# Sparse attention and MoE: value-row transfers between the loads of pairs 2 and 3, `w_in` held back until the last of them, batch 1's preparations late in the first MoE

## The chip, the cores and the metric

The kernel runs on one core of a Trainium2 chip. The metric is the device time of one execution in microseconds. The profile shows one execution taken by the hardware profiler: its span goes from the first to the last instruction, and its own time is a little longer than its span. The engines are called PE (TensorE, matmuls), PEld (its weight loads), DVE (VectorE), ACT (ScalarE), POOL (GpSimd) and SP (SyncE, which here only issues DMAs).

## The reference

Two parts follow each other. First an attention over 4 batches, 8 heads, 768 positions and 64 channels: each query sees the keys within 15 positions of its own, and one summary for each block of 32 keys (the maximum of the keys, the mean of the values).

```python
k_sum = k.reshape(B, H, nb, block, D).max(axis=3)
v_sum = v.reshape(B, H, nb, block, D).mean(axis=3)
scores_l = scale * np.matmul(q, k.transpose(0, 1, 3, 2))      # kept where |i - j| < 16
scores_s = scale * np.einsum('bhsd,bhnd->bhsn', q, k_sum) + np.log(block)
a = softmax(concatenate([masked scores_l, scores_s], -1))
attn_out = np.matmul(a, np.concatenate([v, v_sum], axis=2))
```

Then the heads are laid side by side, x is 3072 tokens by 512, and a feed-forward stage with a swish of learned beta follows:

```python
h = x @ w_in                                   # 512 -> 2048
g = h * (1.0 / (1.0 + np.exp(-beta * h)))
out = g @ w_out                                # 2048 -> 512
```

## The kernel before, in words

**Tiles.** The attention works by batch (4) and pair of heads (4 pairs, called 0 to 3). Queries are taken in tiles of 64; an even tile (parity 0) and an odd one (parity 1) share a window of 128 rows that holds the local keys, and in the rows that are left over the 24 block summaries. So for each pair there are two key arrays in one tile `kw`, and two value arrays, `ve` for the even and `vo` for the odd tiles. Each has 128 partitions, and what lies in its leftover rows must be moved across partitions. This is done by four small DMAs on SP, called the value rows here (L198, L199, L201, L202): 16 rows from `ve` into `vo`, 16 rows from `vo` into `ve`, and the block means `vm` (24 rows) into both.

**Loads.** Batch 0 is loaded as float32 into `hold` tiles by SP and ACT, 384 KB each for k, q and v of a pair (`load3`, L357). Later batches are loaded by GpSimd, which turns them into bf16 on the way, into `st` tiles (192 KB each). The weights `w_in` and `w_out` come by GpSimd in four chunks each of 512 KB in bf16 (`load_w_in`, L342, `load_w_out`, L345). GpSimd also casts or copies every loaded tile (`casts`, L184): k and q into `k_nat` and `q_nat`, v into `ve` and into `vo`.

**The steps of a pair.** `prep_qk` (L208) turns k and q by TensorE into the PSUM tiles `pk` and `pq` (which share two buffers with `vm_ps` and `px`), copies them into `kw` and `q2`, and makes the block maxima `km`. `prep_v` (L191) makes the block means by six matmuls and issues the value rows. `scores` (L244) multiplies queries and keys, takes the exponential on ACT and, from batch 1 on, multiplies by the band on DVE (L264). `av` (L267) multiplies by the values and normalises on DVE (L278, L281). `x_transpose` (L286) turns the result into `xT`.

**The MoE of a batch.** `h_tile` (L301), 16 of them with 8 matmuls each, then `o_part` (L314), 24 of them with 4 matmuls each. `scale_w_out` (L170) divides `w_out` by beta once, on DVE, in 16 instructions of 512 columns. The preparation and the attention of the next batch are put between the tiles of the MoE by `merge` (L327): preparations evenly through the h tiles, scores and `av` through the o parts.

**What sets the order.** SP and GpSimd run in exactly the order of the program. TensorE, DVE and ACT are ordered by the scheduler of the language when the kernel is built, and each runs its list in order. A tile's buffer is reused when its last reader is done. The order on the two hand-ordered queues before the change: on SP all loads of batch 0, then `beta_tmp`, then the value rows of pairs 0 to 3; on GpSimd the casts of pairs 0 to 2, `w_in` chunk 0, the casts of pair 3, three chunks of `w_in`, four of `w_out`, the loads of batch 1's pairs 0 and 1, and then the casts of batch 1.

Of the kernel before, what the change touches and what calls it, by code (L numbers as in the profile page):

```python
# [12 lines left out]
def kernel(  # L13
# [18 lines left out]
    B, H, S, D = q.shape  # L32
    block = 32
    W = 16
    nb = S // block
    QT = 64
    nch = S // P
# [3 lines left out]
    npair = H // 2  # L41
# [120 lines left out]
    beta_tmp = wpool.tile([k2, P], f32, name="beta_tmp")  # L162

    def load_beta():
        beta_ps = ps.tile([P, k2], f32, name="beta_ps", tag="t", bufs=2)
# [4 lines left out]
    def scale_w_out(n):  # L170
        nc.vector.tensor_scalar(out=w_out_sb[:, n], in0=w_out_sb[:, n], scalar1=inv_beta[:, n:n + 1],
                                scalar2=None, op0=ALU.mult)
# [11 lines left out]
    def casts(b, g):  # L184
        nat[(b, g)] = cast_qk("k", b, g), cast_qk("q", b, g)
        ve, vo = ve_bufs[b % 2][:, g], vo_bufs[b % 2][:, g]
        f = staged.pop(("v", b, g)).rearrange("p (h c d) -> p c h d", h=2, d=D)
        nc.gpsimd.tensor_copy(out=ve[:, 0:nch, 0:2 * D].rearrange("p c (h d) -> p c h d", h=2), in_=f)
        nc.gpsimd.tensor_copy(out=vo[:, 1:, 0:2 * D].rearrange("p c (h d) -> p c h d", h=2), in_=f)

    def prep_v(b, g):  # L191
        ve, vo = ve_bufs[b % 2][:, g], vo_bufs[b % 2][:, g]
        vm_ps = ps.tile([P, 2 * D], f32, name="vm_ps", tag="t", bufs=2)
        for c in range(nch):
            nc.tensor.matmul(vm_ps[:], A_avg[:, c, :], ve[:, c, 0:2 * D], start=(c == 0), stop=(c == nch - 1))  # L195
# [105 lines left out]
    def h_tile(b, ni):  # L301
        if ni % 8 == 0:
            h_bufs[(b, ni // 8)] = moe_pool.tile([P, 8, S], bf16, name="h_sb", tag="h_sb", bufs=4)
        big = ps.tile([P, 2, 512], f32, name="h_ps", tag="big", bufs=3)
        for kk in range(2):
            for ki in range(k1):
                nc.tensor.matmul(big[:, kk, 0:MG], w_in_sb[:, ki, ni * P:(ni + 1) * P],  # L307
                                 xT[b][:, ki, kk * MG:(kk + 1) * MG], start=(ki == 0), stop=(ki == k1 - 1))
        nc.scalar.activation(out=h_bufs[(b, ni // 8)][:, ni % 8, :].rearrange("p (k m) -> p k m", k=2),  # L309
                             in_=big[:, :, 0:MG], func=ACTF.Silu, scale=beta_sb[:, ni:ni + 1])  # L310
# [16 lines left out]
    def merge(main, side, span=None):  # L327
        n, m = span or len(main), len(side)
        j = 0
        for i, f in enumerate(main):  # L330
            f()
            while j < m and (j + 1) * n <= (i + 1) * m:
                side[j]()
                j += 1
        while j < m:
            side[j]()
            j += 1

    w_in_r = moe_w_in.rearrange("(a p) n -> p a n", p=P)
    w_out_r = moe_w_out.rearrange("(a p) n -> p a n", p=P)  # L340

    def load_w_in(i, c=d_ff // 4):  # L342
        nc.gpsimd.dma_start(out=w_in_sb[:, :, i * c:(i + 1) * c], in_=w_in_r[:, :, i * c:(i + 1) * c])  # L343
# [16 lines left out]


    load3(0, 2)
    load3(0, 3)
    nc.sync.dma_start(out=beta_tmp[:], in_=moe_beta.rearrange("(a p) -> a p", p=P))
    for g in range(npair):
        casts(0, g)
        if g == 2:
            load_w_in(0)
    for i in range(1, 4):
        load_w_in(i)  # L370
    for i in range(4):
        load_w_out(i)
    prep_qk(0, 0)
    prep_v(0, 0)
    clear_qk(1)
    prep_qk(0, 1)
    both_scores(0, 0)
# [16 lines left out]
    last["norm0"] = last["norm"]  # L394
    load3(1, 0)
    load3(1, 1)

    for b in range(B):
        nxt = b + 1 if b + 1 < B else None
        side_h, side_o = [], []  # L400
        if nxt is not None:
            for g in range(npair):
                def prep(g=g):
                    casts(nxt, g)
                    if g + 2 < npair:
                        load3(nxt, g + 2)
                    prep_qk(nxt, g)
                side_h += [prep, lambda g=g: prep_v(nxt, g)]
# [3 lines left out]
            side_o = list(sc[0])  # L412
            for g in range(1, npair):
                side_o += [sc[g][0], fin[g - 1][0], sc[g][1], fin[g - 1][1], fin[g - 1][2]]
            side_o += fin[npair - 1]
            if nxt + 1 < B:
                side_o[4:4] = [lambda: load3(nxt + 1, 0)]
                side_o[9:9] = [lambda: load3(nxt + 1, 1)]
# [37 lines left out]
```

The softmax here doesn't subtract the row's maximum and nothing guards it: scores larger than these inputs give would overflow.

## Time and profile before

| | |
|---|---|
| median of 3 runs | 262.31 us (261.51 to 264.7) |
| the profiled execution's own time | 263.51 us |
| its span | 261.8 us |
| PE busy | 228.0 us, 87% |
| DVE busy | 153.3 us, 59% |
| ACT busy | 115.6 us, 44% |
| POOL busy | 93.3 us, 36% |
| first stretch of the MoE without waits begins | 50.5 us |
| last piece of batch 1's attention (`px`, TensorE) | 103.05 us |

The busy share of an engine is a mean over stages of different kinds. The first 50 us are the attention of batch 0 alone; from there to about 212 the MoE of batches 0 to 2 runs with the attention of the next batch between its tiles; the rest is the MoE of batch 3. A line of the chain or of a timeline gives the start, the length, the engine, the line of the kernel and the tile written and the tile read; brackets give the idle time before it and what ended it.

### The profile page before, as it was taken

What the parts mean: (1) busy time and instruction counts of PE and PEld (TensorE: products, weight loads), DVE (VectorE), ACT (ScalarE), POOL (GpSimd) and SP (SyncE); (2) the same over time, 40 slices, a digit from 0 to 9 for tenths busy, and PEclk for the clock granted to TensorE, in tenths of its full rate; (3) what the DMA queues carried; (4) which work ended last, traced back from release to release, by engine and by line L of the source; (5) the groups of instructions that cost most, each with busy time, mean ns of one, the idle gap of its engine ahead of it and who ended that gap; (6) DMA issues with size and microseconds to landing.
All of it is one profiled execution on the core that took longest, in us unless ns stands there. A gap on an engine that the chain in (4) does not pass through costs nothing.

```text
span 261.8 us, 4353 instructions
## 1 busy us (share of the span) xinstructions
PE 228.0 (87%) x1681; PEld 138.1 (53%) x1681; DVE 153.3 (59%) x355; ACT 115.6 (44%) x136; POOL 93.3 (36%) x126
## 2 busy tenths in 40 slices
PE   0473866599999879999999999999999999999984
PEld 0262643266665545566665555666655545654431
DVE  7672775669668888266658792666688831001221
ACT  1355641376684320476782331677833306661000
POOL 6679522599999990199510000000000000000000
PEclk9997695789999999999999999999999999999999
DMA  7999999999899999279401111101011111001111
GB/s 180 264 262 148 192 206 201 163 106 112 88 141 148 119 112 155 82 72 119 49 18 74 49 40 62 31 24 25 21 40 71 52 43 40 0 0 43 73 54 73
DMA packets 63667, 24.53 MB, mean 94 GB/s; under 512 B 49808, under 2 KB 60576, under 8 KB 63648
## 3 DMA queue, kind: packets, MB, share of 16 engines
q0 software_dynamic: 41664, 11.28, 42.8%
q1 hardware_dynamic: 18864, 11.82, 16.6%
q10 hardware_dynamic: 3120, 1.18, 2.0%
q8 instruction: 13, 0.21, 0.3%
q14 instruction: 6, 0.05, 0.1%
HBM read 27.27 MB, written 6.29 MB: 128 GB/s over the span
## 4 chain that ended last, share of the span: by engine, by line
PE 68%; DMA 12%; DVE 9%; POOL 5%; SPq 2%; issue 2%; ACT 1%; POOLq 0%; ACTq 0%
PE h_ps L307 32%; PE o_ps L320 25%; DMA st<-in_k_dram 8%; DVE x_nat L281 4%; DMA hold_86<-in_v_dram 4%; DVE attn L264 3%; PE s_ps L259 2%; SPq L83 2%; PE px L292 2%; PE av_ps L276 2%; PE pk L215 2%; PE vm_ps L195 2%; PE pq L235 2%; ACT attn L261 1%; POOL w_in_sb L343 1%
## 5 line engine op out<-in xcount | busy, mean ns | idle before, releaser
L320 PE MATMUL o_ps<-w_out_sb,h_sb 128*128 128x512 bf16 x384 | 92.0, 379 | 0.8 <-DVE o_sb L324 0.8
L307 PE MATMUL h_ps<-xT,w_in_sb 128*128 128x384 bf16 x512 | 91.1, 333 | 0.0
L309 ACT ACTIVATE h_sb<-h_ps,beta_sb 128x768 bf16<-128x768 f32 x64 | 57.5, 900 | 49.8 <-PE h_ps L307 48.9
L307 PEld LDWEIGHTS <-w_in_sb 128*128 128x128 bf16 x512 | 49.8, 99 | 31.6 <-issue 2.0
L320 PEld LDWEIGHTS <-h_sb 128*128 128x128 bf16 x384 | 35.9, 98 | 35.1 <-issue 1.5
L324 DVE COPY o_sb<-o_ps 128x512 f32<-128x512 f32 x24 | 16.6, 690 | 48.7 <-PE o_ps L320 48.4
L261 ACT ACTIVATE attn<-s_ps,bias 128x768 bf16<-128x768 f32 x32 | 28.2, 900 | 34.7 <-PE s_ps L259 26.9
L281 DVE TENSOR_TENSOR x_nat<-av_ps,r 64x384 bf16<-64x384 f32 x64 | 35.5, 555 | 1.5
L276 PEld LDWEIGHTS <-attn 128*128 128x128 bf16 x192 | 14.2, 103 | 16.9 <-issue 6.2
L264 DVE TENSOR_TENSOR attn<-attn,band 128x768 bf16<-128x768 bf16 x24 | 16.1, 671 | 9.9 <-ACT attn L261 9.6
L179 POOL COPY k_nat<-st 128x768 bf16<-128x768 bf16 x12 | 10.9, 908 | 21.5 <-PE pk L215 16.4
L227 DVE TENSOR_REDUCE km<-pk 128x24 bf16<-128x768 bf16 x16 | 15.2, 950 | 5.2 <-ACT kw_139 L225 1.7
L83 POOL DMA_DIRECT2D st<-in_v_dram x12 | 12.5, 1040 | 5.5 <-DMA w_in_sb<-in_moe_w_in_dram 3.2
L215 PEld LDWEIGHTS <-k_nat 128*128 128x128 bf16 x96 | 7.7, 110 | 11.1 <-issue 6.0
L254 PE MATMUL s_ps<-negband,identity 128*128 128x384 bf16 x16 | 6.5, 422 | 7.2 <-DVE negband L129 7.0
L276 PE MATMUL av_ps<-ve_146,attn 128*128 128x129 bf16 x48 | 4.9, 242 | 9.0 <-DMA ve_146<-vm 9.0
L278 DVE RECIPROCAL r<-av_ps 128x6 f32<-128x6 f32 x32 | 6.2, 194 | 10.9 <-PE av_ps L276 10.4
L215 PE MATMUL pk<-identity,k_nat 128*128 128x128 bf16 x96 | 9.3, 239 | 3.1 <-POOL k_nat L179 3.1
L292 PE MATMUL px<-identity,x_nat 128*128 128x128 bf16 x96 | 8.8, 232 | 3.3 <-DVE x_nat L281 2.9
L83 POOL DMA_DIRECT2D st<-in_q_dram x12 | 10.0, 837 | 2.7 <-DMA w_out_sb<-in_moe_w_out_dram 1.8
L235 PE MATMUL pq<-identity,q_nat 128*128 128x128 bf16 x96 | 9.0, 236 | 2.2 <-POOL q_nat L179 1.7
L292 PEld LDWEIGHTS <-x_nat 128*128 128x128 bf16 x96 | 5.9, 103 | 9.4 <-DVE x_nat L281 9.4
(136 smaller groups left out, 240.9 us busy)
## 6 DMA issues: line engine op xcount, KB each, us to landing
out_dram<-o_sb SPq DMA_DIRECT2D x24, 256.0 KB
st<-in_k_dram POOLq DMA_DIRECT2D x12, 192.0 KB, 3.9
st<-in_q_dram POOLq DMA_DIRECT2D x12, 192.0 KB, 4.9
st<-in_v_dram POOLq DMA_DIRECT2D x12, 192.0 KB, 5.7
w_in_sb<-in_moe_w_in_dram POOLq DMA_DIRECT2D x4, 512.0 KB, 8.2
w_out_sb<-in_moe_w_out_dram POOLq DMA_DIRECT2D x4, 512.0 KB, 17.5
hold_84<-in_k_dram SPq DMA_DIRECT2D x3, 384.0 KB
hold_86<-in_v_dram SPq DMA_DIRECT2D x3, 384.0 KB
```

What stands on the lines that cost most here:

```text
L83: eng.dma_start(out=dst, in_=srcs[nm][b, g])
L215: nc.tensor.transpose(pk[:, e, c * P:(c + 1) * P], kt[:, c, e], identity)
L227: nc.vector.tensor_reduce(out=km[:], in_=pk.rearrange("p e (n f) -> p n e f", f=block // NE), op=ALU.max, axis=mybir.AxisListType.XY)
L261: nc.scalar.activation(out=a.rearrange("p (k j) h q -> p k (j h q)", k=2), in_=big[:, :, 0:w], func=ACTF.Exp, bias=bias[:, par:par + 1], s ...
L264: nc.vector.tensor_mul(out=a, in0=a, in1=band[:, par, None, None, :].to_broadcast([P, nch, 2, QT]))
L276: nc.tensor.matmul(ov[:, m // TB, m % TB], a[:, m], vt[:, m], start=True, stop=True)
L281: last["norm"] = nc.vector.tensor_mul(out=x[par * QT:(par + 1) * QT, :, hh, :].rearrange("p (k j) d -> p k j d", k=2), in0=ov[lo:lo + D, : ...
L292: nc.tensor.transpose(px[:, c * P:(c + 1) * P], x[:, c], identity)
L307: nc.tensor.matmul(big[:, kk, 0:MG], w_in_sb[:, ki, ni * P:(ni + 1) * P], xT[b][:, ki, kk * MG:(kk + 1) * MG], start=(ki == 0), stop=(ki = ...
L309: nc.scalar.activation(out=h_bufs[(b, ni // 8)][:, ni % 8, :].rearrange("p (k m) -> p k m", k=2), in_=big[:, :, 0:MG], func=ACTF.Silu, sca ...
L320: nc.tensor.matmul(o_ps, h_bufs[(b, ni // 8)][:, ni % 8, ms * P:(ms + 1) * P], w_out_sb[:, ni, :], start=(ni == 0), stop=(ni == k2 - 1))
L324: nc.vector.tensor_copy(out=o_sb[:], in_=o_ps)
```

## The change

Five things are done.

1. On SP, `beta_tmp` is loaded after the first three loads, and the value rows of pair 0 stand between the loads of pair 2 and the loads of pair 3.
2. On GpSimd, `w_in` chunk 0 is issued after the casts of pair 2, as before; after the casts of pair 3 come `w_in` chunks 1 to 3, then the loads of batch 1's pairs 0 and 1, and the four chunks of `w_out` last (before, `w_out` was ahead of these loads).
3. `w_in` chunk 1 is given a wait for the last value-row transfer of batch 0's pair 3. What follows it on GpSimd follows it in order.
4. `scores` of pairs 2 and 3 of batch 0 are put ahead of `finish` of pairs 0 and 1 in the program.
5. `merge` is replaced by one list of positions. With batch 0's MoE, the four preparations of batch 1 begin at positions 11, 14, 19 and 23 of 40 (16 h tiles, then the scalings of `w_out`, then 24 o parts) in place of one each four h tiles from the start on. With the later MoEs they begin at positions 1, 5, 9 and 13. Scores and `av` stay spread over the first 18 o parts.

```diff
+    beta_tmp = wpool.tile([k2, P], f32, name="beta_tmp")
     load("k", 0, 0, nc.sync)
...
     load("v", 0, 1, nc.scalar)
+    nc.sync.dma_start(out=beta_tmp[:], in_=moe_beta.rearrange("(a p) -> a p", p=P))
...
-        nc.sync.dma_start(out=vo[SUM[1]:SUM[1] + nb, 1:, 0:2 * D], in_=src)
+        last["vw"] = nc.sync.dma_start(out=vo[SUM[1]:SUM[1] + nb, 1:, 0:2 * D], in_=src)
...
     load3(0, 2)
+    for g in range(3):
+        casts(0, g)
+    load_w_in(0)
+    prep_qk(0, 0)
+    prep_v(0, 0)
     load3(0, 3)
-    nc.sync.dma_start(out=beta_tmp[:], in_=moe_beta.rearrange("(a p) -> a p", p=P))
-    for g in range(npair):
-        casts(0, g)
-        if g == 2:
-            load_w_in(0)
-    for i in range(1, 4):
-        load_w_in(i)
+    casts(0, 3)
+    after_vw = [load_w_in(i) for i in range(1, 4)]
+    load3(1, 0)
+    load3(1, 1)
     for i in range(4):
         load_w_out(i)
-    prep_qk(0, 0)
-    prep_v(0, 0)
...
+    both_scores(0, 2)
     finish(0, 0)
-    both_scores(0, 2)
     prep_v(0, 3)
+    tc.add_manual_dep(after_vw[0].ins, last["vw"].ins.name,
+                      mybir.DependencyInfo(mybir.DependencyClass.Sync, mybir.DependencyReason.DATA),
+                      reason="the value rows of batch 0 move ahead of the weights")
+    both_scores(0, 3)
     finish(0, 1)
-    both_scores(0, 3)
...
-    load3(1, 0)
-    load3(1, 1)
...
+            if b == 0:
+                start, step = (11.0, 14.0, k2 + 3.0, k2 + 7.0), 0.5
+            else:
+                start, step = (1.0, 5.0, 9.0, 13.0), 1.0
+            for g in range(npair):
+                side += [(start[g] + step * i, f) for i, f in enumerate(preps[g])]
+            seq = list(sc[0])
             for g in range(1, npair):
-                side_o += [sc[g][0], fin[g - 1][0], sc[g][1], fin[g - 1][1], fin[g - 1][2]]
-            side_o += fin[npair - 1]
+                seq += [sc[g][0], fin[g - 1][0], sc[g][1], fin[g - 1][1], fin[g - 1][2]]
+            seq += fin[npair - 1]
+            side += [(k2 + 1.0 + 18.0 * i / len(seq), f) for i, f in enumerate(seq)]
...
-        merge([lambda ni=ni: h_tile(b, ni) for ni in range(k2)], side_h)
+        main = [lambda ni=ni: h_tile(b, ni) for ni in range(k2)]
         if b == 0:
-            with tc.issue_after(last["norm0"].ins):
-                for n in range(k2):
-                    scale_w_out(n)
-        merge([lambda ms=ms, p=p: o_part(b, ms, p, 4) for ms in range(nch) for p in range(4)],
-              side_o, 18)
+            def scales():
+                with tc.issue_after(last["norm0"].ins):
+                    for n in range(k2):
+                        scale_w_out(n)
+            main.append(scales)
+        main += [lambda ms=ms, p=p: o_part(b, ms, p, 4) for ms in range(nch) for p in range(4)]
+        side.sort(key=lambda z: z[0])
+        for pos, f in enumerate(main):
+            while side and side[0][0] <= pos:
+                side.pop(0)[1]()
+            f()
+        for _, f in side:
+            f()
```

More of the change, by code (lines that the diff above doesn't have):

```diff
@@ L161 @@
     inv_beta = wpool.tile([P, k2], f32, name="inv_beta")
-    beta_tmp = wpool.tile([k2, P], f32, name="beta_tmp")
     def load_beta():
@@ L325, in o_part @@
             nc.sync.dma_start(out=out_r[b * nch + ms], in_=o_sb[:])
[L327 to L337, printed above, removed]
     w_in_r = moe_w_in.rearrange("(a p) n -> p a n", p=P)
@@ L342, in load_w_in @@
     def load_w_in(i, c=d_ff // 4):
-        nc.gpsimd.dma_start(out=w_in_sb[:, :, i * c:(i + 1) * c], in_=w_in_r[:, :, i * c:(i + 1) * c])
+        return nc.gpsimd.dma_start(out=w_in_sb[:, :, i * c:(i + 1) * c], in_=w_in_r[:, :, i * c:(i + 1) * c])
     def load_w_out(i, c=k2 // 4):
@@ L394 @@
     last["norm0"] = last["norm"]
-    load3(1, 0)
-    load3(1, 1)
     for b in range(B):
         nxt = b + 1 if b + 1 < B else None
-        side_h, side_o = [], []
+        side = []
         if nxt is not None:
[L402 to L408, printed above, removed]
+            preps = [[lambda g=g: casts(nxt, g), lambda g=g: prep_qk(nxt, g), lambda g=g: prep_v(nxt, g)]
+                     for g in range(npair)]
+            for g in range(2):
+                preps[g][0:1] += [lambda g=g: load3(nxt, g + 2)]
             sc = [[lambda g=g, u=u: scores(nxt, g, u) for u in range(2)] for g in range(npair)]
@@ L411 @@
                    for g in range(npair)]
-            side_o = list(sc[0])
+            if b == 0:
[5 more added lines that the diff above has]
+            seq = list(sc[0])
             for g in range(1, npair):
-                side_o += [sc[g][0], fin[g - 1][0], sc[g][1], fin[g - 1][1], fin[g - 1][2]]
-            side_o += fin[npair - 1]
+                seq += [sc[g][0], fin[g - 1][0], sc[g][1], fin[g - 1][1], fin[g - 1][2]]
+            seq += fin[npair - 1]
+            side += [(k2 + 1.0 + 18.0 * i / len(seq), f) for i, f in enumerate(seq)]
             if nxt + 1 < B:
-                side_o[4:4] = [lambda: load3(nxt + 1, 0)]
-                side_o[9:9] = [lambda: load3(nxt + 1, 1)]
-        merge([lambda ni=ni: h_tile(b, ni) for ni in range(k2)], side_h)
+                side += [(k2 + 4.0, lambda: load3(nxt + 1, 0)), (k2 + 10.0, lambda: load3(nxt + 1, 1))]
+        main = [lambda ni=ni: h_tile(b, ni) for ni in range(k2)]
         if b == 0:
-            with tc.issue_after(last["norm0"].ins):
-                for n in range(k2):
-                    scale_w_out(n)
-        merge([lambda ms=ms, p=p: o_part(b, ms, p, 4) for ms in range(nch) for p in range(4)],
-              side_o, 18)
+            def scales():
[11 more added lines that the diff above has]
+            f()
 _INS = ['q', 'k', 'v', 'moe_w_in', 'moe_w_out', 'moe_beta']
```

## The prediction

> **What bounds the kernel now.** I read the page first, then the chain of waits in order of time, the table by stretch, the timelines of TensorE, VectorE and GpSimd for the first 110 us, and the groups of single tiles.
>
> From the page, the busy shares:
>
> ```profile
> span 261.8 us, 4353 instructions
> PE 228.0 (87%) x1681; PEld 138.1 (53%) x1681; DVE 153.3 (59%) x355; ACT 115.6 (44%) x136; POOL 93.3 (36%) x126
> ```
>
> TensorE is the bound over the whole, but not everywhere. The chain of waits (start, length, what) shows where it isn't:
>
> ```profile
> 6.76 10.72 DMA hold_86<-in_v_dram
> ...
> 28.16 20.64 DMA st<-in_k_dram
> 48.97 1.48 POOL k_nat L179
> 50.73 3.19 PE h_ps L307 x10
> ...
> 103.05 0.51 PE px L292 x6
> ```
>
> After 50.73 the chain is nearly all TensorE up to the end, with short VectorE pieces at 86 to 99, 144 to 153 and 195 to 211. So what the change can win or lose lies before `px L292` at 103.05: that is the last piece of batch 1's attention, made inside batch 0's MoE, and the later batches follow it like clockwork. I measure everything as a shift of this instant.
>
> The timeline of TensorE (start, length, what, and in brackets the idle time before it with its releaser) shows its waits up to the MoE:
>
> ```profile
> 25.29 0.81 PE L276 MATMUL av_ps<-ve_146,attn 128*128 128x129 bf16 x6 [4.33 <-DMA ve_146<-vm]
> ...
> 40.95 0.81 PE L276 MATMUL av_ps<-ve_146,attn 128*128 128x129 bf16 x6 [3.46 <-DMA ve_146<-vm]
> ...
> 50.50 0.23 PE L215 MATMUL pk<-identity,k_nat 128*128 128x128 bf16 x1 [3.06 <-POOL k_nat L179]
> ```
>
> `av` waits for value rows (9.0 us in three waits, by the table of waits), and the MoE waits until 50.5 for batch 1's first key tile. The timeline of VectorE shows `w_out` scaled just before that, batch 1 begun at 54.34, and in the MoE's second half what casts on GpSimd do to the band multiplication `attn`:
>
> ```profile
> 45.73 4.03 DVE L171 TENSOR_SCALAR w_out_sb<-w_out_sb,inv_beta 128x512 bf16<-128x512 bf16 x15
> 54.34 0.66 DVE L222 COPY kw_138<-pk 128x480 bf16<-128x480 bf16 x1 [4.59 <-PE pk L215]
> ...
> 82.74 0.58 DVE L264 TENSOR_TENSOR attn<-attn,band 128x768 bf16<-128x768 bf16 x1
> ...
> 89.57 2.11 DVE L264 TENSOR_TENSOR attn<-attn,band 128x768 bf16<-128x768 bf16 x1
> ```
>
> The table by stretch (the last two columns are the DMA engines' share and GB/s written) gives the rate of GpSimd's queue, first with weights and then with `st` loads in it:
>
> ```profile
> 30.00:32.00 2.00, 1.10 (x14) 0.80 (x12) 1.17 (x2) 1.99 (x4) 0.76 (x1) 0.97 1.22 201
> ...
> 48.00:50.00 2.00, 0.00 (x0) 0.00 (x0) 1.76 (x7) 0.73 (x1) 1.03 (x1) 1.00 2.09 176
> ```
>
> **What the Trainium skill says.** "DMA: Bandwidth & Descriptors", section Queues, rings and completion order: an engine takes the descriptors of one ring in order, and shares its time by turns among rings. The trace agrees: GpSimd's weights and `st` loads land in the order of issue (`w_in` chunks at 29.9, 33.9 and 37.1, `w_out` at 39.8, 42.9 and up to 47.6, the first `st` at 48.97), and small row transfers take long beside them (issued by 21.6, landed at 25.2). The same page, section Anatomy of one DMA, has a fixed cost of about 2 us; I use that price for rows on a quiet queue, which no row here shows. "SBUF — State Buffer", section Who interferes with whom: a VectorE instruction with two SBUF inputs blocks against a GpSimd instruction that reads SBUF, for its whole length. The `attn` rows agree: 0.58 without, 2.11 with casts running beside it.
>
> **Step 1, rows of pairs 0 to 2.** On SP the four row transfers of pair 0 move ahead of the three loads of pair 3. `vm` is copied at 14.45 to 14.72, so the two that need it issue at 14.8 to 16.5 instead of 20.65 to 22.5, and land by 18.5 instead of 25.2. SP is in order: the three loads queue behind them and issue at 16.5 to 18.1 instead of 10.23 to 16.4. Moved past as well: `beta_tmp`, some 0.6 us earlier on SP, covered by loads in flight.
>
> **Step 2, pair 3 late.** The loads of pair 0 to 2 are 9 x 384 KB; at 265 GB/s from 2.2 us they are over at about 15.6. Pair 3's 1.18 MB start at about 18 and share with `w_in` chunk 0, which GpSimd issues at 17.5: alone they need 4.5 us, with it (2.6 us at 203 GB/s) 7.1. So pair 3's v lands at about 25 (in the kernel before its cast ran at 21.5). TensorE no longer waits for rows at 25.29, but it reaches the `av` of pair 0 at about 25 to 26 anyway, since the built order has all of pair 2's scores and pair 3's transposes ahead of it. The `vm` of pair 3 then follows pair 3's scores and the first `px`: TensorE at 29.8 if the clock stays full, 31.6 at half (before: 33.51).
>
> **Step 3, the hold.** The last row transfer of pair 3 ends its issue at 31.9 to 34.1 and lands 1.8 later, 33.7 to 35.9: middle 34.9. Only then does GpSimd issue `w_in` chunk 1 (before: 23.05). Queued behind it on GpSimd, in this order: two more `w_in` chunks, six `st` loads of batch 1's pairs 0 and 1, four `w_out` chunks, and every cast of batch 1.
>
> **Step 4, the front gain.** Without waits for rows, VectorE paces the end of batch 0's attention: six `av` normalisations of 1.35 (0.20 + 2 x 0.56, with gaps), beta 0.4. From 30.1 to 32.3 that gives 38.7 to 41.2 for the last `px` (before 45.75), and `xT` 0.8 us later. The MoE streams from about 41 rather than 50.5, on `w_in` chunk 0 alone for 32 matmuls; chunk 1, due at 40 to 42, is there in time, since ten matmuls at the half clock (3.35 us, as at 50.56) and 22 at 0.1625 need 6.9 us. By itself this is worth about 8 us (50.5 less 9 matmuls of 0.16 already done is 49.0, against 41).
>
> **Step 5, the queue.** From 34.9, 7 chunks x 0.524 MB and 6 x 0.197 MB are 4.85 MB. At 203 GB/s (rows of 28 to 44 us) 23.9 us, plus 1.0 because `st` loads ran at 176, plus 1.6 to start and 0.7 to finish: the last `w_out` chunk lands at 34.9 + 27.2 = 62.1. Before it landed at about 47.6 (issued 27.4, at most 20.2 to landing). Bounds: 59.5 to 65.
>
> **Step 6, what waits for it.** In the built order of the changed kernel VectorE has all 16 `w_out` scalings ahead of the first copy of batch 1's pair 0. In the kernel before that cost nothing, since `w_out` was there before `k_nat`. Now the last four scalings (0.27 each) end at 63.2 and VectorE stands idle from about 41 to there, but for 12 scalings. TensorE goes on: 90 h matmuls from 41 (10 x 0.32 + 80 x 0.1625) to 57.2, pk and pq 0.7, 14 more 2.3, to 60.2; then the `vm` of batch 1 needs the PSUM buffer of `pk`, which VectorE frees at 63.2 + 1.45 + 0.98 = 65.6. So late preparation is no cover beyond 60.2, and 5.4 us of TensorE go. The shift that decides is VectorE's.
>
> **Step 7, VectorE's stretch.** From the kernel before, start to start: four preparations 5.28 + 5.94 + 4.02 + 4.23 = 19.5; eight `r` with two `x_nat`, 1.37 each, 11.0; eight `attn` at 0.59, 4.7, and 2.7 lost to casts; three `xT` 1.6; four `o_sb` 2.4. Sum 41.9. GpSimd casts through all of it, as before (it now does so from 48 to about 98), so I keep both losses, 3.6 of the copies and 2.7 of `attn`. Added: 1.7 where VectorE waits for TensorE and for an activation table load between pair 1's preparation and the first `attn`, and 5% of the later 28 us, the idle share of VectorE between 78.6 and 103 (23.1 busy of 24.4): 3.1 in all. The stretch is 45.0, between 39 (no losses to casts) and 49.
>
> **Sum.** 63.2 + 45.0 = 108.2 for the last `px`, against 103.05: +5.1. Two o matmuls more stand behind it: +0.4. Later batches: preparations move by about one h tile, 1.3 us, inside stretches where TensorE is the bound: 0. Profiled execution 263.5 + 5.5 = 269.0; the median 262.3 is 1.2 below it, so the forecast for the median is 267.8, say 268.
>
> **Rivals.** (B) Not slower: VectorE's stretch packs tight, because copies and `attn` miss the casts by luck of order. Place: 63 to 103; price 6.3 us; from a stretch of 39.4 downward the time is no longer than before, and at 38.7 it is 261.6. For it: pairs 2 and 3 had only 0.34 and 0.56 for their two copies. Against: casts fill half of the time. (C) Worse: the `vm` rows, the half-speed restart of TensorE after its idle, and PSUM buffers lock VectorE and TensorE together, with 10% idle in place of 5%, and the last `w_out` lands at 65: 275. (D) Faster: the queue, now without rows in it, is quicker, with the last `w_out` at 55 and the gain of step 4 kept: about 255. Against: 201 to 207 GB/s held through 30 to 44 whatever was beside it. The change failing to do what it says (rows not ahead) would need `vm` later than 14.7; nothing earlier moves, so I give it no share.
>
> **Numbers.** Forecast case 0.55 (263 to 272), B 0.25 (258 to 264), C 0.12, D 0.08. 2% of 262.3 is 5.2 us, about what a measurement of this kernel can tell from no change, and the forecast stands just beyond it: slower than that 0.33 of the first case and C, 0.45, rounded up to 0.47 for stalls I can't see; faster D and the low end of B, 0.12; within 0.41. Range 259 to 274.
>
> **What would show it.** Right: row transfers of pair 0 landed by 19; `w_in` chunk 1 issued at 34 to 36; h matmuls streaming from about 41; the last scaling at 61 to 65 with idle time ahead of it put down to `w_out`; TensorE waiting some 5 us near 60; last `px` at 105 to 111. Wrong: `w_out` landed before 57, or the last `px` before 102.

## The result: 3.2% slower, and the profile after

The changed kernel takes 271.43 us (median of 4 runs, 270.15 to 272.94) against 263.13 us before; the ratio is 1.0318 (95% interval 1.023 to 1.0406). Ratios here are formed from undisturbed executions alone, so that a ratio times the time before can lie a little below the median that stands beside it.

From the page of the kernel after, the span, the busy shares and the group of the scalings (its last two parts: busy time and mean, then the idle time before it and what ended it):

```profile
span 271.2 us, 4340 instructions
...
PE 229.8 (85%) x1664; PEld 137.8 (51%) x1681; DVE 153.2 (56%) x355; ACT 115.4 (43%) x136; POOL 93.0 (34%) x126
...
L172 DVE TENSOR_SCALAR w_out_sb<-w_out_sb,inv_beta 128x512 bf16<-128x512 bf16 x16 | 6.9, 497 | 18.1 <-DMA w_out_sb<-in_moe_w_out_dram 18.1
```

No engine has more to do than before: TensorE is busy 229.8 us against 228.0, VectorE 153.2 against 153.3, in a span that is 9.4 us longer. So the loss is waiting, and the third line says for what. The scalings of `w_out`, which had their data early in the kernel before, now hold VectorE idle for 18.1 us.

The chain of waits (start, length, what) shows where that comes from:

```profile
31.92 0.87 SPq L202
32.84 2.34 DMA vo_150<-vm
35.48 2.19 POOL w_in_sb L332 x3
37.67 10.25 DMA st<-in_k_dram
48.20 0.74 POOL w_out_sb L335
49.29 14.66 DMA w_out_sb<-in_moe_w_out_dram
63.98 1.14 DVE w_out_sb L172 x4
65.13 0.66 DVE kw_140 L223
...
66.65 0.88 DVE km L228
67.66 0.80 PE vm_ps L196 x6
68.46 3.20 PE h_ps L308 x10
71.66 0.51 PE pk L216 x6
...
110.56 0.46 PE px L293 x6
```

Read it downwards. The last value-row transfer of pair 3 lands at about 35.2 and GpSimd issues the other three `w_in` chunks; the queue then brings `w_in`, `st` and `w_out` one after the other until about 64; four scalings follow; only then comes the first copy of batch 1, `kw_140` at 65.13. From there the chain goes over to TensorE: `vm`, ten h matmuls at 0.32 us each (0.16 before the stop), and `pk` of pair 1. In the kernel before, the first copy of batch 1 stood at 54.34 and the last `px` of batch 1 at 103.05; here that `px` is at 110.52.

The table of waits (total, times, longest) names the three waits on this path:

```profile
DVE w_out_sb L172 <- DMA w_out_sb<-in_moe_w_out_dram: 18.1, 3, 16.2
...
PE vm_ps L196 <- DVE km L228: 9.9, 2, 8.5
...
POOL w_in_sb L332 <- DMA vo_150<-vm: 9.4, 1, 9.4
```

And the timeline of VectorE (idle time before an instruction in brackets) shows the place:

```profile
56.27 4.57 DVE L172 TENSOR_SCALAR w_out_sb<-w_out_sb,inv_beta 128x512 bf16<-128x512 bf16 x8 [16.20 <-DMA w_out_sb<-in_moe_w_out_dram]
...
63.98 1.14 DVE L172 TENSOR_SCALAR w_out_sb<-w_out_sb,inv_beta 128x512 bf16<-128x512 bf16 x4 [1.33 <-DMA w_out_sb<-in_moe_w_out_dram]
65.13 0.66 DVE L223 COPY kw_140<-pk 128x480 bf16<-128x480 bf16 x1
...
72.20 0.66 DVE L223 COPY kw_141<-pk 128x480 bf16<-128x480 bf16 x1 [2.67 <-PE pk L216]
...
76.98 3.82 DVE L265 TENSOR_TENSOR attn<-attn,band 128x768 bf16<-128x768 bf16 x3 [0.76 <-ACT attn L262]
```

VectorE stands idle from 40 to 56 with the whole preparation of batch 1 behind the scalings in its list. TensorE runs h matmuls without a break meanwhile, from 41.96, and stops at 59.2 for 8.5 us, since `vm` needs a PSUM buffer that VectorE has not emptied. VectorE in its turn waits 2.67 us at 72.20 for the `pk` of pair 1, which stands behind that stop.

### The profile page after: what moved, and what is told of

Its sections match the earlier page's. It is cut to its first block, busy times and chain, and to the rows that moved or that the text cites. A ratio compares the mean times of both kernels' runs of the same rounds, so it can differ in the third digit from the quotient of the medians.

```text
span 271.2 us, 4340 instructions
## 1 busy us (share of the span) xinstructions
PE 229.8 (85%) x1664; PEld 137.8 (51%) x1681; DVE 153.2 (56%) x355; ACT 115.4 (43%) x136; POOL 93.0 (34%) x126
## 3 DMA queue, kind: packets, MB, share of 16 engines
q0 software_dynamic: 41664, 11.28, 41.1%
## 4 chain that ended last, share of the span: by engine, by line
PE 57%; DVE 17%; DMA 13%; ACT 7%; issue 3%; POOL 1%; SPq 0%; ACTq 0%; POOLq 0%
PE h_ps L308 25%; PE o_ps L321 21%; DVE x_nat L282 6%; DMA w_out_sb<-in_moe_w_out_dram 5%; DMA st<-in_k_dram 4%; ACT attn L262 4%; DVE attn L265 3%; DMA hold_85<-in_q_dram 3%; PE s_ps L260 2%; PE vm_ps L196 2%; PE px L293 2%; DVE o_sb L325 2%; PE pq L236 2%; PE pk L216 2%; PE av_ps L277 1%
## 5 line engine op out<-in xcount | busy, mean ns | idle before, releaser
L282 DVE TENSOR_TENSOR x_nat<-av_ps,r 64x384 bf16<-64x384 f32 x64 | 35.5, 554 | 1.4
L265 DVE TENSOR_TENSOR attn<-attn,band 128x768 bf16<-128x768 bf16 x24 | 15.5, 654 | 8.9 <-ACT attn L262 8.5
L180 POOL COPY k_nat<-st 128x768 bf16<-128x768 bf16 x12 | 10.5, 874 | 23.5 <-PE pk L216 20.0
L277 PEld LDWEIGHTS <-attn 128*128 128x128 bf16 x192 | 13.2, 99 | 10.0 <-issue 3.7
L172 DVE TENSOR_SCALAR w_out_sb<-w_out_sb,inv_beta 128x512 bf16<-128x512 bf16 x16 | 6.9, 497 | 18.1 <-DMA w_out_sb<-in_moe_w_out_dram 18.1
L196 PEld LDWEIGHTS <-A_avg 128*128 128x128 bf16 x96 | 6.3, 104 | 18.7 <-issue 12.2
L196 PE MATMUL vm_ps<-ve_149,A_avg 128*128 128x128 bf16 x48 | 4.3, 230 | 9.9 <-DVE km L228 9.9
L293 PEld LDWEIGHTS <-x_nat 128*128 128x128 bf16 x96 | 6.5, 107 | 10.3 <-DVE x_nat L282 9.7
L180 POOL COPY q_nat<-st 128x768 bf16<-128x768 bf16 x12 | 10.5, 874 | 0.4 <-DMA st<-in_q_dram 0.2
```

The source lines that it names most:

```text
L180: last["cast"] = nc.gpsimd.tensor_copy(out=t[:], in_=f)
L265: nc.vector.tensor_mul(out=a, in0=a, in1=band[:, par, None, None, :].to_broadcast([P, nch, 2, QT]))
L277: nc.tensor.matmul(ov[:, m // TB, m % TB], a[:, m], vt[:, m], start=True, stop=True)
L282: last["norm"] = nc.vector.tensor_mul(out=x[par * QT:(par + 1) * QT, :, hh, :].rearrange("p (k j) d -> p k j d", k=2), in0=ov[lo:lo + D, : ...
L293: nc.tensor.transpose(px[:, c * P:(c + 1) * P], x[:, c], identity)
```

## The experiments

The theory, called A in the expectations, is that of the prediction: the front of the kernel does get faster, but the hold delays the weight queue, the 16 scalings wait for that queue at the head of VectorE's list, and the end of batch 1's attention is as late as VectorE's first copy (the runs below change this last clause). Its rivals put the loss into the late positions of the preparations, or into the order of the queue, or (called F) say that from the first `attn` on the pace is the same whatever is done before. All times are medians; the kernel before stood at 263.1 to 263.3 us in these comparisons.

### Which part of the change costs

**Without the hold.** The one wait of `w_in` chunk 1 is taken out; all else is the changed kernel.

```diff
-    tc.add_manual_dep(after_vw[0].ins, last["vw"].ins.name, ...)
```

> The changed kernel without the wait of w_in chunk 1 for the last value-row transfer; order of queues and placement stay. Theory A: w_in chunk 1 issues at about 26 instead of 35.5, the last w_out chunk lands at about 55, so the scalings are over before the first pk; the rows of pair 3 land slower (5 us beside weights instead of 2), so the MoE streams from about 44 instead of 42, first copy at about 59, last px at 102 to 105, time 262 to 266. Rival B' (the hold pays for itself: without it the rows cost as much as in the kernel before, MoE from 47): 266 to 269. Rival C: 269 or more.

Measured: 263.04 us, ratio 1.0009 (0.9966 to 1.0052). The whole loss is gone. On VectorE's timeline the last scalings and the first copy stand about 8 to 9 us earlier:

```profile
54.75 1.14 DVE L172 TENSOR_SCALAR w_out_sb<-w_out_sb,inv_beta 128x512 bf16<-128x512 bf16 x4 [1.41 <-DMA w_out_sb<-in_moe_w_out_dram]
...
57.37 0.66 DVE L223 COPY kw<-pk 128x480 bf16<-128x480 bf16 x1 [1.48 <-PE pk L216]
...
62.40 0.66 DVE L223 COPY kw<-pk 128x480 bf16<-128x480 bf16 x1 [0.38 <-PE pk L216]
```

TensorE no longer waits at `vm`, and the last `px` is at 101.07. What the hold was buying: without it, the rows of pair 3 share the DMA engines with the weights, and `av` waits for them once, 2.5 us; the MoE then streams from 42.70 and not from 41.96. Over the changed kernel and all its variants below, the MoE streams from 41.7 to 42.7 in the four profiles with the hold and from 42.7 to 43.8 in the seven without it. So the hold wins about 1 us at the front, and costs 8.4 us at the end.

**Without the scalings.** The 16 scalings are left out, so the output lacks the factor 1/beta; the hold stays.

```diff
             def scales():
-                with tc.issue_after(last["norm0"].ins):
-                    for n in range(k2):
-                        scale_w_out(n)
+                pass
```

> The changed kernel without the 16 scalings of w_out by 1/beta on VectorE (left out: the division by beta, so the output lacks it); all transfers, the hold and the placement stay. Theory A (VectorE stands still behind the scalings until the last w_out chunk lands near 64): the first copy of batch 1's pair 0 starts at about 57 instead of 65.1, TensorE no longer waits 8.5 us before vm, the last px comes at 100 to 103 instead of 110.5, and the time is 261 to 264. Rival B (the hold on w_in costs by itself, through loads and casts that come late): the first copy still starts after 63, time 269 or more. Rival C (preparation begun at position 11 is too late in any case, the VectorE stretch grows when packed): first copy at 57, but last px not before 107, time 267 or more.

Measured: 261.25 us (258.25 to 263.92 in four executions), ratio 0.9814 (0.9741 to 0.9886), last `px` at 100.11. A was right. VectorE's first copy, with the hold still in place:

```profile
57.41 0.66 DVE L223 COPY kw<-pk 128x480 bf16<-128x480 bf16 x1 [16.62 <-PE pk L216]
```

VectorE is idle about as long as in the changed kernel, but now only because TensorE does not reach `pk` sooner; nothing behind it is late. The work of the 16 instructions is a small part of the gain: in the changed kernel 12 of them ran inside the idle time, and only the last four, 1.14 us, stand between the landing and the first copy. So the hold hurts through the instructions that wait for its queue on VectorE. The two kernels without the hold and without the scalings have the same first copy (57.37 and 57.41) and the last `px` within 1 us.

**`w_out` ahead of the `st` loads.** The hold stays; on GpSimd's queue `w_out` is put back in front of batch 1's loads.

```diff
-    load3(1, 0)
-    load3(1, 1)
     for i in range(4):
         load_w_out(i)
+    load3(1, 0)
+    load3(1, 1)
```

> The changed kernel with the four w_out chunks ahead of the six st loads of batch 1 on GpSimd, as in the kernel before; the hold stays. Theory A: the last w_out chunk lands at about 57, the scalings are over by 59, and the first copy of pair 0 waits for the st load and its cast instead, at about 61; last px at 105 to 107, time 266 to 268: part of the loss, as something else in the same queue is late now. Rival B (the hold decides, not who is behind it): 270 to 272. Rival C: 270 to 272.

Measured: 268.55 us, ratio 1.0174 (1.0128 to 1.022). The last scalings start at 57.62, 6.4 us earlier than in the changed kernel, but the first copy comes only 4.5 us earlier, at 60.67. TensorE's timeline says why:

```profile
59.81 0.82 PE L216 MATMUL pk<-identity,k_nat 128*128 128x128 bf16 x6 [2.86 <-POOL k_nat L180]
```

The wait for weights has become a wait for batch 1's keys, which now stand last in the same queue. The time and the last `px` (107.11) lie just above what A had. Whichever of the two is last in the queue is late, once the queue starts at 36.

**Only the late positions.** The kernel before, with batch 1's preparations at 11, 14, 19 and 23; later batches, queues and loads as before.

```diff
-        merge([lambda ni=ni: h_tile(b, ni) for ni in range(k2)], side_h)
...
+            start = (11.0, 14.0, k2 + 3.0, k2 + 7.0)
+            for g in range(npair):
+                side += [(start[g] + 0.5 * i, f) for i, f in enumerate(prep_of(g))]
+            side += [(k2 + 1.0 + 18.0 * i / len(side_o), f) for i, f in enumerate(side_o)]
...
```

> The kernel before with only batch 1's preparations moved to positions 11, 14, 19 and 23 of the first MoE; queues, rows and the later batches as before. Theory A (the end of batch 1's attention is VectorE's first copy plus a stretch of 43 to 46 us, so starting late costs whatever it saves in waits): the MoE streams from 47.4 without the wait for k_nat, the first copy comes at about 65 instead of 54.3, the last px at 108 to 111, time 268 to 271. Rival D (late placement wins the 3.1 us wait for k_nat and the rest is hidden): 259 to 262.

Measured: 269.79 us, ratio 1.0244 (1.0164 to 1.0323). Late positions alone cost about 6.5 us. TensorE's timeline:

```profile
49.65 0.29 PE L215 MATMUL pk<-identity,k_nat 128*128 128x128 bf16 x1 [4.02 <-POOL k_nat L179]
...
54.52 0.44 PE L215 MATMUL pk<-identity,k_nat 128*128 128x128 bf16 x5
...
66.84 0.51 PE L195 MATMUL vm_ps<-ve,A_avg 128*128 128x128 bf16 x6
```

And VectorE's first copies of pairs 0 and 1:

```profile
55.00 0.66 DVE L222 COPY kw<-pk 128x480 bf16<-128x480 bf16 x1 [6.10 <-PE pk L215]
...
71.62 0.66 DVE L222 COPY kw<-pk 128x480 bf16<-128x480 bf16 x1 [2.07 <-PE pk L215]
```

The scheduler still pulled all of `pk` of pair 0 forward, so the wait for `k_nat` is not even removed and the first copy is at 55.00, not at about 65 as A had it. Only `vm` (66.84) and pair 1 (71.62) come at their late places, and the first `attn` at 76.40. Two preparations then share VectorE with the scores, and the last `px` is at 109.77. So A had the time and the end right, but not by the first copy, from which it now takes 54.8 us to the end.

**Only the early rows.** The kernel before, with pair 0's value rows (and `beta_tmp`) ahead of pair 3's loads.

```diff
+    for g in range(3):
+        casts(0, g)
+    load_w_in(0)
+    prep_qk(0, 0)
+    prep_v(0, 0)
     load3(0, 3)
+    casts(0, 3)
...
-    prep_qk(0, 0)
-    prep_v(0, 0)
```

> The kernel before with only the value rows of pair 0 (and beta) ahead of the loads of pair 3 on SP; order of GpSimd's queue, placement and program order of scores as before, no hold. Theory A: rows of pair 0 land by 19, but w_in chunk 1 issues at about 26 instead of 23, so the first st load lands 1 to 2 us later than 48.97 and the MoE, which waits for it, streams from 51 to 52; last px at 103 to 105, time 263 to 265: no gain. Rival E (rows are what the front waits for): 257 to 260.

Measured: 262.69 us, ratio 1.0016 (0.9986 to 1.0046): no gain, as expected (A had 263 to 265). In its profile batch 0's last `px` starts at 41.1 (45.75 before), and TensorE then waits 7.8 us for `k_nat`. That profiled execution was 4.5 us above the median, so how long the wait is in the median one stays open; that the gain is not in the time is shown.

These runs split the change. Early rows alone: nothing. Late positions alone: +6.5 us. All of it without the hold: nothing, since a MoE that streams from 42.7 in place of 50.5 makes good what the late positions cost (last `px` at 101.07 against 109.77 with late positions alone). The hold: +8.4 us on top.

One distance holds through all kernels so far that have the late positions: from VectorE's first copy of pair 1 to the last `px`. It is 38.3 us in the changed kernel (72.20 to 110.52), 38.7 without the hold (62.40 to 101.07), 37.7 without the scalings (62.44 to 100.11), 38.7 with `w_out` ahead (68.43 to 107.11) and 38.2 with late positions alone (71.62 to 109.77). From the first copy of pair 0 it is anything from 42.7 to 54.8. Pair 1's copy needs the `pk` of pair 1, which stands in TensorE's stream of h matmuls: 19.7 us after the stream's start where nothing stops the stream (42.70 to 62.40 without the hold), 30.2 in the changed kernel (41.96 to 72.20). The 10.5 us between the two are the stop of 8.46 at `vm` and about 2 for the slow matmuls after it. So the loss runs from the hold over `w_out`, the scalings and the first copy into a stop of TensorE, and through that stop to the end.

### Can the wait be moved out of the way

**Scalings behind pair 1.** The changed kernel with its hold; the scalings may issue only after pair 1's `vm` copy, whose instruction is kept in `last`.

```diff
-        nc.vector.tensor_copy(out=vm[:], in_=vm_ps[0:nb])
+        last[("vm", b, g)] = nc.vector.tensor_copy(out=vm[:], in_=vm_ps[0:nb])
...
-                with tc.issue_after(last["norm0"].ins):
+                with tc.issue_after(last[("vm", 1, 1)].ins):
```

> The changed kernel with the 16 scalings put behind the preparation of batch 1's pair 1 in VectorE's order; nothing left out. Theory A: preparations of pairs 0 and 1 run from 57 to about 66, the scalings (4.5 to 6 us) then hardly wait for w_out, the first band multiplication is at about 70 to 72 instead of 77, last px at 103 to 106, time 263 to 267. Rival B: no change, 270 to 272. Rival C: at most 2 us won, since the packed stretch of 45 us stays and only its start moves: 269 or more.

Measured: 273.18 us, ratio 1.0352 (1.0306 to 1.0398). A was wrong by 6 us or more, and only the range of C holds the time. Pairs 0 and 1 were prepared by 65.35, as A said, but then VectorE's timeline reads:

```profile
65.35 9.90 DVE L172 TENSOR_SCALAR w_out_sb<-w_out_sb,inv_beta 128x512 bf16<-128x512 bf16 x16
75.17 3.35 DVE L265 TENSOR_TENSOR attn<-attn,band 128x768 bf16<-128x768 bf16 x3
...
93.30 3.57 DVE L231 COPY kw<-km 128x144 bf16<-128x144 bf16 x2
```

Their data was there; the 16 scalings took 9.90 us beside GpSimd's work for pairs 2 and 3 (casts from 65.2 to 69.9, issues of three `st` loads from 69.86 to 72.60, casts again), where 15 of them took 4.03 us in the kernel before. The first copy had come 8.75 us earlier (56.38 against 65.13), and the scalings, now inside the stretch, took more than that back: the last `px` is at 110.65, 49.2 us behind the first copy of pair 1, and 9.9 of these are the scalings. The answer for the tile `w_out_sb` (shortest, median and longest in ns) shows the single instructions:

```profile
L172 DVE TENSOR_SCALAR w_out_sb<-w_out_sb,inv_beta x16: 335/851/974, 65.4 to 74.3; 128x512 bf16<-128x512 bf16 x16
```

The median of 851 ns is about the length of one cast, 830 ns. The long ones don't lie beside casts alone: of the four that began while GpSimd issued the `st` loads, three took 798 to 908 ns. The scaling that the kernel before had at 59.55, 679 ns, lay beside such issues too. For the casts this agrees with what the Trainium skill says in "SBUF — State Buffer", section Who interferes with whom: VectorE's `tensor_scalar` can use the port pair that it shares with GpSimd, and whoever has the pair keeps it for a whole instruction. The first `attn` is at 75.17 and not 76.98, and the two copies at 93.30 then take 3.57 us beside further casts.

**Preparations spread evenly, no hold.** Positions 1, 5, 9 and 13 for batch 1 too; scalings where the built order has them, first on VectorE.

```diff
-    tc.add_manual_dep(...)
...
-            if b == 0:
-                start, step = (11.0, 14.0, k2 + 3.0, k2 + 7.0), 0.5
-            else:
-                start, step = (1.0, 5.0, 9.0, 13.0), 1.0
+            start, step = (1.0, 5.0, 9.0, 13.0), 1.0
```

> The changed kernel without the hold and with batch 1's preparations at positions 1, 5, 9 and 13; VectorE's built order has 12 scalings ahead of pair 0's copies and 4 behind. Theory A: chunk 2 of w_out lands at about 52, the first copy starts at about 54 (57.4 with late placement), the last px at 98 to 100, time 260 to 262. Rival F (the late placement is needed, since early preparations take the TensorE and the port at a bad time): 264 or more.

Measured: 269.7 us, ratio 1.0224 (1.0129 to 1.0319). A miss: its rival was right. TensorE's timeline shows the longest wait:

```profile
56.98 0.80 PE L196 MATMUL vm_ps<-ve,A_avg 128*128 128x128 bf16 x6 [7.60 <-DVE km L228]
```

Early in the program, `vm` of pair 0 stands early in TensorE's list too, and while VectorE still waits for `w_out`, the h matmuls behind `vm` stand as well, 7.6 us. The late positions of the change protect against just this: without the hold and with the late positions TensorE has no such wait.

**The same, scalings behind pair 1.**

```diff
-                with tc.issue_after(last["norm0"].ins):
+                with tc.issue_after(last[("vm", 1, 1)].ins):
```

> As the kernel without the hold and with preparations at 1, 5, 9 and 13, with the 16 scalings behind the preparation of batch 1's pair 1 in VectorE's order (6 there, 10 behind pair 2). Theory A: st loads are there from 40, so the first copy starts at 46 to 48; the stretch is 44 plus 4 to 10 for the scalings that now lie in it beside casts; last px at 94 to 101, time 256 to 262, the low end if the scalings take 0.3 each, the high end if 0.6. Rival F: 264 or more.

Measured: 266.18 us, ratio 1.0071 (1.004 to 1.0102). Again a miss, and F was right. The first copy comes at 46.81 as expected. In the profile TensorE then waits 4.4 us for `k_nat` of pair 2, whose load lands at about 61 because it is issued behind `w_out`. That profiled execution was 4 us above the median, so this wait is a sign and no measure.

**Three mixtures.** From the two misses I drew a condition: no preparation may stand in TensorE's list before its loads have landed, and no scaling before its weights have, nor beside casts. In the kernel without the hold pairs 0 and 1 are cast from 40 and from 46 on (in `mix_a` from 43 and from 49), `w_out` is there at about 54.7, and pair 2 can be cast only from 56 (60) on. All three kernels are without the hold. In `mix_a` the scalings follow pair 1:

```diff
-                start, step = (11.0, 14.0, k2 + 3.0, k2 + 7.0), 0.5
+                start, step = (1.0, 5.0, 13.0, k2 + 5.0), 0.5
...
-                with tc.issue_after(last["norm0"].ins):
+                with tc.issue_after(last[("vm", 1, 1)].ins):
```

> The changed kernel without the hold, batch 1's preparations at positions 1, 5, 13 and 21 of 40, and the 16 scalings behind the preparation of pair 1 in VectorE's order. Theory A (what costs is a VectorE that stands still ahead of its stretch, and a preparation in front of the h stream that has to wait): the first copy comes at 46 to 48 as with the even positions; pair 2, now at 13, finds its keys loaded (about 62), so TensorE has no wait over 1 us in the h stream, the first attn starts at 68 to 72 and the last px ends at 97 to 101: 257 to 261 us. Rival F (from the first attn on it is pace by pace the same, and whatever is done early is lost again to scalings and copies beside GpSimd's casts): the last px at 104 to 108, 263 us or more.

Measured: 261.25 us, ratio 0.9902 (0.9873 to 0.993): 1.0% below the kernel before and about 4% below the changed one. The gain over the kernel before is small, and this is the best of five tries, but its interval lies below 1. Expected were 257 to 261, so it stands at the upper end. VectorE's timeline:

```profile
46.55 0.66 DVE L223 COPY kw<-pk 128x480 bf16<-128x480 bf16 x1 [4.59 <-PE pk L216]
...
55.59 4.30 DVE L172 TENSOR_SCALAR w_out_sb<-w_out_sb,inv_beta 128x512 bf16<-128x512 bf16 x16
...
69.94 1.88 DVE L265 TENSOR_TENSOR attn<-attn,band 128x768 bf16<-128x768 bf16 x2
```

The scalings fall into a gap of GpSimd (no cast and no issue between 54.9 and 60.1) and take 4.30 us, all 16 between 331 and 352 ns (one starts every 0.26 us, before the one ahead of it has ended). No wait of TensorE in the h stream is over 0.5 us, and the last `px` is at 99.42, 3.6 us earlier than in the kernel before. Of that, 2.0 are lost again in the later batches (below); this kernel with the old positions there was not run.

`mix_c` has the positions 2, 7, 12 and 21, with the scalings behind pair 0 (`last[("vm", 1, 0)]`):

> The changed kernel without the hold, batch 1's preparations at positions 2, 7, 12 and 21 of 40, and the 16 scalings behind the preparation of pair 0 in VectorE's order. Theory A: the first copy at 47 to 49, the scalings run when the last w_out has landed (about 54.5) and end at 57 to 60 depending on the casts beside them, pair 1 follows, no wait of TensorE above 2 us, the last px at 98 to 102: 258 to 262 us. Rival F: the scalings take 8 us or more beside the casts, pair 1's vm is waited for by TensorE for 3 us or more, the last px at 104 to 108: 263 us or more.

Measured: 267.49 us, ratio 1.01 (1.0064 to 1.0135), with single executions from 263.5 to 270.2. The profiled one took 264.2 us and has what A said, the first copy at 45.87 and the last `px` at 101.81, but also a wait of TensorE of 3.1 us at `vm`. The time sides with F, the trace more with A (its scalings took 5.2 us and not 8). Why the time varies so much is open.

`mix_d` has the positions 8, 11, 14 and 21 and the scalings first:

> The changed kernel without the hold, with batch 1's preparations at positions 8, 11, 14 and 21 of 40; the 16 scalings stay ahead of the first copy, where the built order has them. Theory A: the first copy stays at 57 (the last w_out lands at about 54.5), the vm of pair 0 comes no earlier in TensorE's order than the kernel without the hold has it by more than 3 h tiles, so TensorE waits at vm for some 3 us, but three preparations are over before the first attn: the last px at 98 to 101, 260 to 263 us. Rival F: the wait at vm costs what the third preparation wins, the last px at 102 to 105, 264 to 267 us.

Measured: 265.25 us, ratio 1.012 (1.0084 to 1.0156). F was right. TensorE's timeline has the wait that both theories expected, 3.85 us for some 3:

```profile
60.92 0.76 PE L196 MATMUL vm_ps<-ve,A_avg 128*128 128x128 bf16 x6 [3.85 <-DVE km L228]
```

and the third preparation ahead of the first `attn`, now at 74.90 (67.18 without the hold at the change's own positions), wins nothing back. So of the three only `mix_a` bears the condition out.

### The later batches

**Old positions in the later batches.** Without the hold, batch 1 late, but batches 2 and 3 at the positions of the kernel before.

```diff
-    tc.add_manual_dep(...)
...
-            if b == 0:
-                start, step = (11.0, 14.0, k2 + 3.0, k2 + 7.0), 0.5
-            else:
-                start, step = (1.0, 5.0, 9.0, 13.0), 1.0
+            start, step = (11.0, 14.0, k2 + 3.0, k2 + 7.0), 0.5
             for g in range(npair):
-                side += [(start[g] + step * i, f) for i, f in enumerate(preps[g])]
+                if b == 0:
+                    side += [(start[g] + step * i, f) for i, f in enumerate(preps[g])]
+                else:
+                    side += [(o + (2.0 if i == len(preps[g]) - 1 else 0.0), f) for i, f in enumerate(preps[g]) for o in [2.0 + 4.0 * g]]
```

> The changed kernel without the hold, with the preparations of batches 2 and 3 back at the positions of the kernel before (2, 6, 10, 14, with prep_v two h tiles behind) in place of 1, 5, 9 and 13; batch 1's stay late. Theory A (the new positions of the later batches are where about 1 us is lost between the end of batch 1's attention and batch 3's MoE): 1 us less than the kernel without the hold, 261.5 to 262.5 us, and the distance from the last px of batch 1 to the first h matmul of batch 3 shrinks by about 1 us. Rival (the later positions cost nothing, the 1 us comes from the clock or from what batch 1 leaves over): 262.7 to 263.5 us.

Measured: 262.92 us, ratio 0.9975 (0.9936 to 1.0013), against 1.0009 (0.9966 to 1.0052) with the new positions. The time does not tell them apart. The profiles do: from the last `px` of batch 1 to the unbroken h matmuls of batch 3 it takes 113.20 us in the kernel before, 115.17 in the changed one, 115.14 without the hold and 114.23 here. These small differences can be trusted: in all ten profiles with the new positions in the later batches it is 115.14 to 115.20, whatever batch 1 did, and with only the rows early it is 113.20 as before. So the new positions of the later batches account for about 0.9 of the 2.0 us. In this run's profile batch 1 ended 0.9 us later than in the one without the hold, so that the total was the same; it was behind from the front on, where `av` waited 3.24 us for rows in place of 2.52 and the MoE streamed from 43.75 in place of 42.70.

## Why the prediction was right, and which terms were mis-sized

The forecast was 268 us, with slower as the likeliest of the three outcomes, though only at 0.47 against 0.41 for no clear change; measured are 271.4, inside the range. The mechanism is the one of steps 3 to 6, and removing either end of it (the hold, or the scalings that wait) removes the loss. Its size was taken too small: 5.5 us of span, where 9.4 came. The terms, by the prediction's own steps:

| step | predicted | measured |
|---|---|---|
| 1, rows of pair 0 that need `vm` issue from | 14.8 | 14.76 |
| 2, v of pair 3 cast; `vm` of pair 3 on TensorE | 25; 29.8 to 31.6 | 24.5; 30.5 |
| 3, `w_in` chunk 1 issued | 34.9 | 35.5 |
| 4, MoE streams from | 41 | 41.96 |
| 5, last `w_out` chunk landed | 62.1 | about 64.0 |
| 6, first copy of batch 1 on VectorE | 63.2 | 65.1 |
| 6, wait of TensorE at `vm` | 5.4 | 8.5 |
| 7, from there to the last `px` | 45.0 | 45.4 |
| last `px` of batch 1 | 108.2 | 110.5 |
| from there to batch 3, more than before | 0.4 | 2.0 |
| span, more than before | 5.5 | 9.4 |

Steps 1 to 4 hold within a microsecond; the last row transfer of pair 3 landed 1.5 us after its issue had ended (33.7 to 35.2), where step 3 had 1.8. (The price of about 2 us, from the Trainium skill, "DMA: Bandwidth & Descriptors", section Anatomy of one DMA, is given there for DMAs that GpSimd issues, and the rows are SP's.) **Step 5** was too short: 0.6 from a hold that ended later than the middle I took, and 1.3 from the queue, which needed 28.5 us from the issue to the landing for which I had 27.2. Its bounds, 59.5 to 65, hold it. **Step 6** followed it by 1.9 us; the TensorE wait was longer by more than that, since TensorE also arrived at 59.2 and not 60.2. The step says that the shift that decides is VectorE's; the chain shows that TensorE's stop is part of the path, since VectorE waits for what stands behind it at 72.20. **Step 7** came out at 45.4, but this closeness is luck, since two parts of the sum were wrong and nearly cancel. VectorE's waits in the stretch are 6.1 us (2.7 at `kw` of pair 1, 72.20, and 1.8 at `xT`, 92.18, are the longest, both for TensorE), where the sum had 3.1. The idle share of 5% behind that was a misreading: the table by stretch has VectorE busy for 21.45 of the 24.4 us from 78.6 to 103 in the kernel before, not for 23.1, which is 12% idle; in the changed kernel it is 13% from 82.5 to 110.5. Losses to casts are 4.0 us (2.1 in the three `attn` at 76.98, 3.82 less 3 x 0.59, and 1.9 in the copies `kw<-km`, of which 1.3 at 84.12), where the sum had 6.3. **The last term** was simply wrong: I put the later batches at 0 (plus 0.4), and they lost 2.0, of which 0.9 is due to their new positions and the rest is not explained. The three terms, 1.9 + 0.4 + 1.6, are the 3.9 us by which the span missed.

Of the rivals, B (not slower) needed a stretch of 39.4 or less; it was 45.4. D (faster) needed `w_out` at 55; it came at 64. C was nearest to the landing (65), and its slow restart and its lock over PSUM buffers are in the trace; but the idle share of 10% that it expected in place of 5% was there before the change, the stretch came out only 0.4 us longer than the forecast had it, and its 275 was not reached.

Step 4 said that the front alone is worth about 8 us. No run shows it in the time by itself: with early rows alone it is not there. Without the hold it is there, and pays for the late positions: 8.7 us at the last `px` (109.77 with late positions alone, 101.07), of which 6.75 are left in the time (269.79, 263.04), as the later batches take about 2 of them.

## What to carry to other kernels

When a transfer at the head of an in-order queue is given a wait, work out when the last transfer behind it lands and who stands first in line for that: here about 1 us won at the front cost 8.4 us behind it, through 16 short instructions at the head of another engine's list. When such instructions are moved, look what the new place lies beside; the same 16 took 4.3 us in a gap of GpSimd's work and 9.9 us among it. An interleaved preparation stood best just behind the landing of its own data, neither earlier (it stopped the stream around it) nor much later (the work after it was squeezed together); of three mixtures built on this, one gained. And look for the point from which the distance to the end stays the same in every variant; here it was not the first copy of the stretch but the first of pair 1, and that led to the engine that held everything up.

## What the runs showed of the hardware that was not expected

A run of 128x512 bf16 `tensor_scalar` instructions on VectorE went at 0.27 us each with GpSimd idle and at 0.62 us each beside casts of 0.83 us and the issues of loads between them, with single ones of up to 0.97. The prediction had priced this for `attn` and for the copies `kw<-km`, and not for the scalings, though one of 0.68 us stood in its own timeline. Two copies `kw<-km` of 128x144, 0.30 us when alone, took up to 3.57. Also, rows issued beside the weight queue cost TensorE only one wait of 2.5 us (2.2 to 3.2 in the other profiles without the hold that show it), less than the 8.4 us that the hold cost.
